# Group normalisation on one core: loops that begin at tile 0, padding on SyncE, and a sixth load cut into four gated parts

## The chip, the core and the metric

The kernel runs on one core of one Trainium2 chip. The metric is the device time of one execution in microseconds (us). The kernel before has a median of 633.02 us over three runs, between 632.91 and 633.99 us. A profile was taken of one further execution; the pages and the trace below are from it.

## What is computed

The input `x` has the shape 128 x 1024 x 32 x 16 in bf16. The 1024 channels of each of the 128 samples form 32 groups of 32 channels. Each group of each sample is normalised by its own mean and variance, and each channel is then scaled and shifted:

```
xr  = x.reshape(B, 32, C // 32, H, W)
mu  = xr.mean(axis=(2, 3, 4), keepdims=True)
var = ((xr - mu) ** 2).mean(axis=(2, 3, 4), keepdims=True)
xn  = ((xr - mu) / sqrt(var + 1e-5)).reshape(B, C, H, W)
out = xn * g[None, :, None, None] + b[None, :, None, None]
```

A group is 32 x 512 = 16,384 numbers, so one partition holds one group of one sample in one row of 32 KB, and 128 partitions hold the 32 groups of four samples.

## The kernel before, in words

The work is 32 tiles of 128 x 16,384 bf16 (4 MB each). Six buffers `xt0` to `xt5` hold them; tile i lives in buffer i mod 6, is normalised in place and is stored from there. Three small tables of ones, an identity matrix and a replication matrix are made at the start, and `g` and `b` (2 KB each) are loaded by ScalarE's queue and spread over the partitions by one small matmul (L143).

Each tile passes through the engines in this order. TensorE (PE) waits for the load (`ld[j]`, L155) and adds the 32 pieces of 512 columns with 32 matmuls against the identity (L157), which leaves 512 partial sums per row. VectorE (DVE) reduces them to minus the mean (`mean`, L176). ScalarE (ACT) squares the centred row in two halves with a running sum (L270, the two halves of one tile), and makes the standard deviation in two small instructions (L284, L291). VectorE inverts it (L189), forms scale and shift per channel (L192, L199), and applies them in 32 instructions of 512 columns (L209). VectorE runs `mean` one tile ahead: in the step of tile i it first does `mean(i + 1)`, then waits for the standard deviation of tile i.

SyncE (SP) issues every large transfer on one queue, in an order written out by hand (L112 to L139). It issues loads 0 to 5, then a *spacer* (`spacer`, L113 to L120: a load of 32 columns of 128 rows into a tile that nobody reads, 8 KB). Then it issues the stores in order, each after a wait for VectorE (`s_dve`). After stores 1, 4, 7, ... 25 it issues the next two or three loads, each after a wait for the store that frees its buffer (`st[j]`, L125), and after each such group one more spacer, which also waits for the spacer before it. In the steady part the queue thus holds, over and over, three stores, three loads and a spacer. There are 32 loads, 32 stores and 10 spacers. SyncE's program is written out in full, without a loop.

The other three engines run a loop of their own each (`loop`, L93 to L109). Tiles 0 and 1 (`HEAD = 2`) are written out ahead of it; then come five passes of six tiles. `head_slot={engine: 0}` puts the first instruction of the loop's body at the start of a block of the instruction memory; the engine jumps to it. At the end of a pass each engine waits until its own work has settled and takes the semaphores back by the pass's counts.

The lines that the change touches are the order of SyncE's queue (L111 to L139), the loop helper (L93 to L109), the waits' counts in the steps (L152 to L297), and the last wait for the spacers (L309).

Of the kernel before, what the change touches and what calls it, by code (L numbers as in the profile page):

```python
# [17 lines left out]
NBUF = 6  # L18
RUN = 3
MM_FREE = 512  # L20
HEAD = 2
SPARE = 32


@with_exitstack
def kernel(
# [7 lines left out]
    nc = tc.nc  # L34
    P = nc.NUM_PARTITIONS
# [6 lines left out]
    NT = B0 // NS  # L42
    KC = C // G
    F = KC * HW
    inv_n = 1.0 / float(F)
    NMM = F // MM_FREE
    TRIPS = (NT - HEAD) // NBUF
    assert F % MM_FREE == 0 and HEAD + TRIPS * NBUF == NT

    x_v = x.rearrange("(t n) (g k) h w -> t (n g) (k h w)", n=NS, g=G)  # L50
    o_v = out.rearrange("(t n) (g k) h w -> t (n g) (k h w)", n=NS, g=G)
# [6 lines left out]
    xt = [sb.tile([P, F], BF16, name=f"xt{j}") for j in range(NBUF)]  # L58
# [20 lines left out]
    def sem(name):  # L79
        return tc.alloc_semaphore(name)  # L80

    ld = [sem(f"ld{j}") for j in range(NBUF)]
    st = [sem(f"st{j}") for j in range(NBUF)]
    s_gb, s_set, s_eye, s_rep = sem("s_gb"), sem("s_set"), sem("s_eye"), sem("s_rep")
    s_pe, s_mean, s_sq, s_std = sem("s_pe"), sem("s_mean"), sem("s_sq"), sem("s_std")
    s_spare = sem("s_spare")
# [3 lines left out]
        j = i % NBUF  # L90
        return t[:, j : j + 1]

    def loop(engine, step, settle, counts):  # L93


        for i in range(HEAD):
            step(i)
        with nc.Fori(
            0,
            TRIPS,  # L100
            1,
            engines=bass.OrderedEngineSet([engine.engine]),
            head_slot={engine.engine: 0},
        ):
            for i in range(HEAD, HEAD + NBUF):
                step(i)
            settle()
            for s, n in counts:
                engine.sem_inc(s, -n)  # L109

    spacers = [0]  # L111

    def sync_program(sync):  # L113
        def spacer():

            n = spacers[0]
            spacers[0] += 1
            if n:
                sync.wait_ge(s_spare, 16 * n)
            sync.dma_start(out=spare[:], in_=x_v[0][:, 0:SPARE]).then_inc(s_spare, 16)  # L120

        def load(i):
            j = i % NBUF
            if i >= NBUF:
                sync.wait_ge(st[j], 16 * (i // NBUF))  # L125
            sync.dma_start(out=xt[j][:], in_=x_v[i]).then_inc(ld[j], 16)

        for i in range(min(NBUF, NT)):
            load(i)
        spacer()  # L130
        for i in range(NT):
            j = i % NBUF
            sync.wait_ge(s_dve, i + 1)
            sync.dma_start(out=o_v[i], in_=xt[j][:]).then_inc(st[j], 16)
            if (NT - NBUF - 1 - i) % RUN == 0 and i < NT - NBUF:
                for n in range(max(NBUF, i + 1 + NBUF - RUN), min(i + 1 + NBUF, NT)):
                    load(n)
                spacer()

    def tensor_program(pe):  # L140
        pe.wait_ge(s_gb, 32)
        pe.wait_ge(s_rep, 1)
        pe.matmul(  # L143
            out=gb_p[:].rearrange("p a k -> p (a k)"),
            lhsT=rep[:],
            rhs=gb_b[:].rearrange("q a k -> q (a k)"),
            start=True,
            stop=True,
        ).then_inc(s_pe, 1)
        pe.wait_ge(s_eye, 1)  # L150

        def step(i):  # L152
            j = i % NBUF
            pe.wait_ge(ld[j], 16)
            pe.sem_inc(ld[j], -16)  # L155
            for k in range(NMM):
                m = pe.matmul(  # L157
                    out=pa[j][:],
                    lhsT=eye[:],
                    rhs=xt[j][:, k * MM_FREE : (k + 1) * MM_FREE],  # L160
                    start=(k == 0),
                    stop=(k == NMM - 1),
                )
            m.then_inc(s_pe, 1)

        loop(pe, step, lambda: None, [])
        pe.drain()
        pe.sem_inc(s_pe, 1)

    def vector_program(dve):  # L170
        dve.memset(ones_b[:], 1.0).then_inc(s_set, 1)  # L171
        dve.tensor_copy(out=gb[:], in_=gb_p[:])._wait_ge(s_pe, 1).then_inc(s_dd, 1)  # L172
        gam, bet = gb[:, 0, :], gb[:, 1, :]

        def mean(i):
            dve.tensor_scalar(  # L176
                out=jd[i % 2][:],
                in0=pa[i % NBUF][:],
                scalar1=-inv_n,
                scalar2=None,  # L180
                op0=ALU.mult,
                op1=ALU.add,
                accum_out=col(negmean, i),
            )._wait_ge(s_pe, i + 2).then_inc(s_mean, 1)

        def step(i):
            j = i % NBUF
            mean(i + 1)
            dve.reciprocal(out=col(rstd, i), in_=col(std, i))._wait_ge(  # L189
                s_std, i + 1  # L190
            ).then_inc(s_dd, 1)
            dve.tensor_scalar(  # L192
                out=scl[j][:],
                in0=gam,
                scalar1=col(rstd, i),
                scalar2=None,
                op0=ALU.mult,
            )._wait_ge(s_dd, 3 * i + 2).then_inc(s_dd, 1)
            dve.scalar_tensor_tensor(  # L199
                out=bia[j][:],  # L200
                in0=scl[j][:],
                scalar=col(negmean, i),
                in1=bet,
                op0=ALU.mult,
                op1=ALU.add,
            )._wait_ge(s_dd, 3 * i + 3).then_inc(s_dd, 1)
            for k in range(KC):
                span = xt[j][:, k * HW : (k + 1) * HW]
                m = dve.tensor_scalar(  # L209
                    out=span,  # L210
                    in0=span,
                    scalar1=scl[j][:, k : k + 1],
                    scalar2=bia[j][:, k : k + 1],
                    op0=ALU.mult,
                    op1=ALU.add,
                )
                if k == 0:
                    m._wait_ge(s_dd, 3 * i + 4)
                if k == KC - 2 and i == HEAD + NBUF - 1:
                    m.then_inc(s_dd, 1)  # L220
            m.then_inc(s_dve, 1)

        def settle():
            dve.wait_ge(s_dd, 3 * (HEAD + NBUF) + 2)

        mean(0)
        loop(
            dve,
            step,
            settle,  # L230
            [(s_pe, NBUF), (s_std, NBUF), (s_dd, 3 * NBUF + 1)],
        )

    def pool_program(pool):
# [26 lines left out]
    def scalar_program(act):  # L261
        act.dma_start(out=gb_b[:, 0, :], in_=g_v).then_inc(s_gb, 16)
        act.dma_start(out=gb_b[:, 1, :], in_=b_v).then_inc(s_gb, 16)
        act.wait_ge(s_set, 2)
        act.activation(out=warm[:], in_=eps_t[:], func=ACT.Sqrt)  # L265

        def step(i):
            j = i % NBUF
            for h in range(2):
                m = act.activation(  # L270
                    out=ja[:],
                    in_=xt[j][:, h * F // 2 : (h + 1) * F // 2],
                    func=ACT.Square,
                    bias=col(negmean, i),
                    scale=1.0,
                    accum_out=sq[:, 2 * j + h : 2 * j + h + 1],
                    saturate=False,
                )
                if h == 0:
                    m._wait_ge(s_mean, i + 1)  # L280
                else:
                    m._wait_ge(s_sq, 3 * i + 1)
                m.then_inc(s_sq, 1)
            act.activation(  # L284
                out=col(half, i),
                in_=sq[:, 2 * j : 2 * j + 1],
                func=ACT.Identity,
                bias=eps_t[:],
                scale=inv_n,
            )._wait_ge(s_sq, 3 * i + 1).then_inc(s_sq, 1)  # L290
            act.activation(  # L291
                out=col(std, i),
                in_=sq[:, 2 * j + 1 : 2 * j + 2],
                func=ACT.Sqrt,
                bias=col(half, i),
                scale=inv_n,
            )._wait_ge(s_sq, 3 * i + 3).then_inc(s_std, 1)  # L297

        loop(act, step, lambda: act.drain(), [(s_mean, NBUF), (s_sq, 3 * NBUF)])

    with tc.tile_critical():  # L301
        with nc.Block() as block:
            block.sync(sync_program)
            block.tensor(tensor_program)
            block.vector(vector_program)
            block.gpsimd(pool_program)
            block.scalar(scalar_program)

        nc.sync.wait_ge(s_spare, 16 * spacers[0])  # L309
        for j in range(NBUF):  # L310
            nc.sync.wait_ge(st[j], 16 * len(range(j, NT, NBUF)))

# [29 lines left out]
```

## Time and profile before

| | |
|---|---|
| median of three runs | 633.02 us |
| the profiled execution, its own time | 633.55 us |
| its span, first to last instruction | 631.8 us |
| ACT busy | 476.2 us (75%) |
| DVE busy | 375.7 us (59%) |
| PE busy | 262.4 us (42%) |
| bytes moved by the DMA engines | 268.61 MB, a mean of 425 GB/s over the span |
| share of the DMA engines' time on the queue of the loads and stores (q1) | 99.0% |

The profile is one page of parts and a trace behind it that can be asked for views. In the page, part 2 cuts the span into 40 slices of 15.8 us; a digit is the busy share of a slice in tenths. Part 3 lists the DMA queues. Queues marked *instruction* carry pieces of the engines' programs. Part 6 lists transfers by line with the median time from issue to landing. The views used below are the timeline of one engine or queue, the waits of SyncE's queue, a table of stretches of time with the DMA engines' share in each, and the DMA queues in one stretch. The trace also keeps the completion marks of the transfers: a transfer leaves sixteen, one from each DMA engine that took part, with the time of each.

### The profile page before, as it was taken

What the parts mean: (1) busy time and instruction counts of PE and PEld (TensorE: products, weight loads), DVE (VectorE), ACT (ScalarE), POOL (GpSimd) and SP (SyncE); (2) the same over time, 40 slices, a digit from 0 to 9 for tenths busy, and PEclk for the clock granted to TensorE, in tenths of its full rate; (3) what the DMA queues carried; (4) which work ended last, traced back from release to release, by engine and by line L of the source; (5) the groups of instructions that cost most, each with busy time, mean ns of one, the idle gap of its engine ahead of it and who ended that gap; (6) DMA issues with size and microseconds to landing.
All of it is one profiled execution on the core that took longest, in us unless ns stands there. A gap on an engine that the chain in (4) does not pass through costs nothing. (4 is left out here: it accounts for less than half of the span.)

```text
span 631.8 us, 3680 instructions
## 1 busy us (share of the span) xinstructions
PE 262.4 (42%) x1025; PEld 106.8 (17%) x1025; DVE 375.7 (59%) x1188; ACT 476.2 (75%) x194; POOL 0.9 (0%) x7
## 2 busy tenths in 40 slices
PE   1987409009602850573077019404730680095000
PEld 0333103003200320231032003101310230032000
DVE  0057477775772677077727745771777177447771
ACT  0496999997994599289919964993899199749930
POOL 0000000000000000000000000000000000000000
PEclk9978858658855985687579559955975786598555
DMA  9999999999999999999999999999999999999986
GB/s 365 430 432 416 434 436 428 434 432 431 428 432 431 432 432 431 434 424 432 432 431 430 438 434 428 436 434 434 428 440 432 434 432 436 431 432 428 432 386 289
DMA packets 10760, 268.61 MB, mean 425 GB/s; under 512 B 2560, under 2 KB 2560, under 8 KB 2560
## 3 DMA queue, kind: packets, MB, share of 16 engines
q1 hardware_dynamic: 10656, 268.52, 99.0%
q8 instruction: 2, 0.03, 0.0%
q14 instruction: 6, 0.05, 0.0%
q10 hardware_dynamic: 96, 0.00, 0.0%
HBM read 134.30 MB, written 134.22 MB: 425 GB/s over the span
## 5 line engine op out<-in xcount | busy, mean ns | idle before, releaser
L270 ACT ACTIVATE ja<-xt,negmean 128x8192 fp8e5<-128x8192 bf16 x64 | 455.5, 7117 | 127.3 <-DVE jd L176 121.3
L157 PE MATMUL pa<-xt,eye 128*128 128x512 bf16 x1024 | 262.2, 421 | 307.4 <-PEq L155 305.2
L209 DVE TENSOR_SCALAR xt<-xt,scl,bia 128x512 bf16<-128x512 bf16 x1024 | 333.7, 407 | 1.2
L157 PEld LDWEIGHTS pa<-xt,eye 128*128 128x128 bf16 x1024 | 106.7, 106 | 462.5 <-issue 369.9
L176 DVE TENSOR_SCALAR_CACHE_REDUCE jd<-pa 128x512 bf16<-128x512 f32 x33 | 22.7, 687 | 143.5 <-PE pa L157 141.8
L189 DVE RECIPROCAL rstd<-std 128x1 f32<-128x1 f32 x32 | 5.2, 162 | 83.7 <-ACT std L291 83.7
L270 ACT ACTIVATION_READ_ACCUMULATOR ja<-xt,negmean 128x1 f32 x64 | 11.9, 186 | 0.0
L291 ACT ACTIVATE std<-sq,half 128x1 f32<-128x1 f32 x32 | 9.4, 295 | 1.0
L284 ACT ACTIVATE half<-sq,eps_t 128x1 f32<-128x1 f32 x32 | 8.9, 278 | 0.0
L199 DVE SCALAR_TENSOR_TENSOR bia<-scl,negmean,gb 128x32 f32<-128x32 f32 x32 | 8.1, 252 | 1.1
L192 DVE TENSOR_SCALAR scl<-gb,rstd 128x32 f32<-128x32 f32 x32 | 7.7, 242 | 1.1
L172 DVE COPY gb<-gb_p 128x64 f32<-128x64 f32 x1 | 0.2, 225 | 10.2 <-PE gb_p L143 10.2
L143 PE MATMUL gb_p<-gb_b,rep 32*128 32x64 bf16 x1 | 0.2, 228 | 11.2 <-DMA gb_b<-in_b_dram 11.2
L176 DVE DVE_READ_ACCUMULATOR jd<-pa 128x1 f32 x33 | 2.7, 83 | 0.0
L265 ACT ACT_TABLE_LOAD x1 | 1.3, 1283 | 1.9 <-issue 1.9
L143 PEld LDWEIGHTS gb_p<-gb_b,rep 32*128 32x128 bf16 x1 | 0.1, 97 | 11.2 <-DMA gb_b<-in_b_dram 11.2
L171 DVE MEMSET ones_b<- 128x128 bf16 x1 | 0.2, 165 | 1.1 <-SPq L301 1.1
L244 POOL TENSOR_SCALAR_AFFINE_SELECT rep<-ones_b 32x128 bf16<-32x128 bf16 x1 | 0.3, 302 | 0.0
L235 POOL TENSOR_SCALAR_AFFINE_SELECT eye<-ones_b 128x128 bf16<-128x128 bf16 x1 | 0.3, 293 | 0.8 <-DVE ones_b L171 0.8
L265 ACT ACTIVATE warm<-eps_t 128x1 f32<-128x1 f32 x1 | 0.2, 203 | 0.0
L253 POOL TENSOR_SCALAR eps_t<-ones_b 128x1 f32<-128x1 bf16 x1 | 0.2, 203 | 0.0
L326 POOL MEMSET const-bfloat16-1.0<- 128x1 bf16 x1 | 0.1, 102 | 0.0
(3 smaller groups left out, 0.3 us busy)
## 6 DMA issues: line engine op xcount, KB each, us to landing
xt<-in_x_dram SPq DMA_DIRECT2D x32, 4096.0 KB, 29.1
out_dram<-xt SPq DMA_DIRECT2D x32, 4096.0 KB, 33.0
spare<-in_x_dram SPq DMA_DIRECT2D x10, 8.0 KB, 29.1
gb_b<-in_g_dram ACTq DMA_DIRECT2D x1, 2.0 KB, 6.5
gb_b<-in_b_dram ACTq DMA_DIRECT2D x1, 2.0 KB, 9.7
```

The costliest lines, as they stand in the source:

```text
L143: pe.matmul(out=gb_p[:].rearrange("p a k -> p (a k)"), lhsT=rep[:], rhs=gb_b[:].rearrange("q a k -> q (a k)"), start=True, stop=True,).the ...
L157: m = pe.matmul(out=pa[j][:], lhsT=eye[:], rhs=xt[j][:, k * MM_FREE : (k + 1) * MM_FREE], start=(k == 0), stop=(k == NMM - 1),)
L176: dve.tensor_scalar(out=jd[i % 2][:], in0=pa[i % NBUF][:], scalar1=-inv_n, scalar2=None, op0=ALU.mult, op1=ALU.add, accum_out=col(negmean, i),
L189: dve.reciprocal(out=col(rstd, i), in_=col(std, i))._wait_ge(s_std, i + 1).then_inc(s_dd, 1)
L192: dve.tensor_scalar(out=scl[j][:], in0=gam, scalar1=col(rstd, i), scalar2=None, op0=ALU.mult,)._wait_ge(s_dd, 3 * i + 2).then_inc(s_dd, 1)
L199: dve.scalar_tensor_tensor(out=bia[j][:], in0=scl[j][:], scalar=col(negmean, i), in1=bet, op0=ALU.mult, op1=ALU.add,)._wait_ge(s_dd, 3 * i ...
L209: m = dve.tensor_scalar(out=span, in0=span, scalar1=scl[j][:, k : k + 1], scalar2=bia[j][:, k : k + 1], op0=ALU.mult, op1=ALU.add,)
L235: pool.affine_select(out=eye[:], in_=ones_b[:], pattern=[[-1, P]], compare_op=ALU.is_equal, fill=0.0, base=0, channel_multiplier=1,)._wait ...
L265: act.activation(out=warm[:], in_=eps_t[:], func=ACT.Sqrt)
L270: m = act.activation(out=ja[:], in_=xt[j][:, h * F // 2 : (h + 1) * F // 2], func=ACT.Square, bias=col(negmean, i), scale=1.0, accum_out=s ...
L284: act.activation(out=col(half, i), in_=sq[:, 2 * j : 2 * j + 1], func=ACT.Identity, bias=eps_t[:], scale=inv_n,)._wait_ge(s_sq, 3 * i + 1) ...
L291: act.activation(out=col(std, i), in_=sq[:, 2 * j + 1 : 2 * j + 2], func=ACT.Sqrt, bias=col(half, i), scale=inv_n,)._wait_ge(s_sq, 3 * i + ...
```

## The change

Four things change together.

1. `HEAD` goes. The three loops begin with tile 0, make five passes of six tiles, and tiles 30 and 31 are written out behind them. The waits count by the position in the pass. Only VectorE's loop keeps `head_slot`; those of TensorE and ScalarE begin wherever their program stands.
2. Load 5 is issued as four loads of 32 rows (rows c, c + 4, c + 8, ...; 1 MB each). Parts 0 and 1 are issued at once; part 2 waits until part 0 has landed, part 3 until part 1 has landed, and SyncE goes on only when part 2 has landed. A semaphore `ld_x` tells TensorE that the other parts are in; it is raised after every load into buffer 5.
3. Between parts 1 and 2 SyncE increments an otherwise unused semaphore 28 times (`PAD`).
4. The spacers go, all but one behind load 5.

```diff
-HEAD = 2
+PAD = 28
...
-    TRIPS = (NT - HEAD) // NBUF
+    TRIPS = (NT - 1) // NBUF
+    LOOPED = TRIPS * NBUF
...
-    def loop(engine, step, settle, counts):
-        for i in range(HEAD):
-            step(i)
+    def loop(engine, step, settle, counts, aligned=False):
         with nc.Fori(
...
-            head_slot={engine.engine: 0},
+            **({"head_slot": {engine.engine: 0}} if aligned else {}),
         ):
-            for i in range(HEAD, HEAD + NBUF):
-                step(i)
+            for j in range(NBUF):
+                step(j, j)
             settle()
             for s, n in counts:
                 engine.sem_inc(s, -n)
+        for i in range(LOOPED, NT):
+            step(i, i - LOOPED)
...
             sync.dma_start(out=xt[j][:], in_=x_v[i]).then_inc(ld[j], 16)
+            if j == NBUF - 1:
+                sync.sem_inc(ld_x, 1)
+
+        def load_gated(i):
+            j = i % NBUF
+            for c in range(4):
+                if c == 2:
+                    for n in range(PAD):
+                        sync.sem_inc(s_pad, 1)
+                if c >= 2:
+                    sync.wait_ge(qt[c - 2], 16)
+                rows = slice(c, P, 4)
+                sync.dma_start(out=xt[j][rows], in_=x_v[i][rows]).then_inc(
+                    qt[c] if c < 3 else ld[j], 16
+                )
+            sync.wait_ge(qt[2], 16)
+            sync.sem_inc(ld_x, 1)
 
-        for i in range(min(NBUF, NT)):
+        for i in range(NBUF - 1):
             load(i)
-        spacer()
+        load_gated(NBUF - 1)
+        sync.dma_start(out=spare[:], in_=x_v[0][:, 0:SPARE]).then_inc(s_spare, 16)
...
                     load(n)
-                spacer()
...
             pe.wait_ge(ld[j], 16)
             pe.sem_inc(ld[j], -16)
+            if j == NBUF - 1:
+                pe.wait_ge(ld_x, 1)
+                pe.sem_inc(ld_x, -1)
...
-        loop(pe, step, lambda: None, [])
-        pe.drain()
-        pe.sem_inc(s_pe, 1)
```

The last two lines gave VectorE's `mean(32)` its count; in the changed kernel `mean` is called only for tiles that exist, so VectorE does 32 of them in place of 33. The order of the loads and stores in the queue, the six buffers, the groups of three and every operation on a tile are the same.

## The prediction

> **What bounds the kernel now.** I read the page's slices first. The compute rows are far from full (ACT, the busiest, 75%), while the DMA row is full to the last two slices:
>
> ```profile
> DMA  9999999999999999999999999999999999999986
> GB/s 365 430 432 416 434 436 428 434 432 431 428 432 431 432 432 431 434 424 432 432 431 430 438 434 428 436 434 434 428 440 432 434 432 436 431 432 428 432 386 289
> ```
>
> So the stream of 64 transfers of 4 MB is the work to count. Its clean pace comes from the timeline of SyncE's queue, where the first load of each group is issued when a store has landed:
>
> ```profile
> 289.84 19.67 SPq L126 DMA_DIRECT2D xt<-in_x_dram  x3
> ...
> 348.02 19.64 SPq L126 DMA_DIRECT2D xt<-in_x_dram  x3
> ...
> 406.18 19.69 SPq L126 DMA_DIRECT2D xt<-in_x_dram  x3
> ...
> 465.17 19.68 SPq L126 DMA_DIRECT2D xt<-in_x_dram  x3
> ```
>
> Three stores, three loads and a spacer take 58.18 and 58.16 us, then 58.99: 9.695 us a transfer when clean (58.17 / 6), and 0.8 us lost once. 64 x 9.695 = 620.5 us. The first data packet starts at 2.05, so a stream without loss would land at 622.5. The last store lands at 630.3, where SyncE's last wait ends:
>
> ```profile
> SPq L311 <- DMA out_dram<-xt: 11.5, 1, 11.5
> ```
>
> (it began at 618.8). Some 7.8 us are lost, and the table of stretches, whose last three columns are granted clock, DMA share and GB/s, tells how:
>
> ```profile
> 600.00:612.00 12.00, 0.00 (x0) 0.00 (x0) 8.82 (x29) 6.42 (x4) 0.00 (x0) 0.50 1.00 431
> 612.00:618.50 6.50, 0.00 (x0) 0.00 (x0) 5.68 (x18) 0.00 (x0) 0.00 (x0) 0.50 0.46 197
> 618.50:628.30 9.80, 0.00 (x0) 0.00 (x0) 0.00 (x0) 0.00 (x0) 0.00 (x0) 0.50 1.00 429
> ```
>
> From 612 to 618.5 more than half of the 16 DMA engines are idle while the rest still carry store 30. The engines have drifted apart, and the last one sets each landing. The completion marks give the drift. Take the mark of each engine less 2.05 + 9.695 x (place in the queue), in us:
>
> ```
>                 load 0  load 2  load 4  load 5  load 7  load 10  load 13  load 16  load 22  load 25  load 29  load 31  store 30
> median engine    1.32    1.36    1.39    2.03    2.13    2.14     2.13     2.09     2.06     2.06     1.95     1.99     1.93
> last engine      1.77    3.07    3.11    4.54    4.59    5.51     5.56     6.50     6.61     7.39     7.38     7.73     7.78
> ```
>
> The median engine loses nothing after load 5. The last one loses 1.30 at load 2, 1.43 at load 5, and then 0.92, 0.94, 0.78 and 0.35 at loads 10, 16, 25 and 31: each time the last load of a group, when the engines ahead already write the next store. The loss at load 2 is a piece of TensorE's program, fetched as it reaches its loop; this is the queue part of the stretch 30.9 to 32.2 us:
>
> ```profile
> q1 hardware_dynamic: 31, 0.59, 108.0%
> q8 instruction: 1, 0.02, 4.8%
> ```
>
> 4.8% of 16 engines x 1.3 us is 1.0 us, all on one engine. A second such piece comes at 69.5 us, pieces of 8 KB (0.31 us each) at 57.4, 58.8, 63.9, 65.9, 115.4 and 622.5; these hit engines that were not last.
>
> **The change, part by part.** All terms are for the last engine, since it sets the end.
>
> *Spacers.* Nine go. On each engine a spacer is 8 packets of 11 ns and a mark of 9 ns: 97 ns, 9 x 0.097 = 0.87 us, in a queue that never rests. Bounds 0 and -0.87; I take **-0.87**. Their issue (0.43 us of SyncE each) costs nothing, as SyncE waits 367 us for VectorE in all.
>
> *The gate.* A part is two rows per engine, 2 x 1.213 us (the packet's duration in the trace) = 2.43 us. When part 0 has landed on the last engine, part 1 is already queued there. From a packet's end to its mark is 0.35 us, from mark to SyncE's next issue 0.02 (74.50 to 74.52 at the first gated load of before), from issue to first packet 1.0 (1.0 to 2.02 at load 0): 1.4 us, under 2.43. So the last engine does not rest: **0**. If that cover were gone, each of the three gates could cost it what is over 2.43. The engines ahead do rest, and come out at most 2.43 - 1.4 = 1.1 us ahead, where they were 2.5 ahead at load 5. SyncE stands in the gates until about 61 us; behind it stand the spacer and store 0, which VectorE has ready at 50.6. Store 0 lay behind load 5 in the queue anyway (it lands at 74.5, a store's 9.7 us after load 5's 64.8), so the later issue is hidden as long as load 5 takes no longer.
>
> *What the level field saves.* The four later losses sum to 0.92 + 0.94 + 0.78 + 0.35 = 2.99. Engines within about 1 us of the median lost nothing at those switches, and the field starts inside that. Bounds 0 and -2.99; I keep 0.4 for the drift that returns: **-2.6**. At load 5 itself the median engine lost 0.64 and the last 1.43; level engines should lose what the median did: **-0.8** (bounds 0 and -1.43).
>
> *Fetches.* TensorE's 16 KB piece stays: TensorE still reaches its second block while loads run, and 1.30 on one engine remains: **0** (bounds -1.30 if it meets an early engine and +1.30 if a second one falls behind the gate). ScalarE's pieces go with its jump. They cost it this:
>
> ```profile
> 59.14 7.12 ACT L270 ACTIVATE ja<-xt,negmean 128x8192 fp8e5<-128x8192 bf16 x1 [4.96 <-issue]
> ```
>
> but ScalarE's 5 us were hidden, since store 1 could not start before store 0 ended at 74: **0**. VectorE's two, and SyncE's (moved by the 28 increments to about 5 us, while loads 0 and 1 run), go ahead of the gate, which levels them. Behind it I allow one 8 KB piece, as the 622.5 us one: **+0.3**.
>
> *Small steps.* SyncE's increments of `ld_x`, TensorE's wait for it (raised before the load lands) and one `mean` less (0.69 us) lie under waits of tens of us: **0**.
>
> Sum: -0.87 - 2.6 - 0.8 + 0.3 = -4.0 us. The profiled execution had 633.55 us (span 631.8); it would be 629.55. The median lies 0.53 below the profiled execution, so I forecast **629.0**.
>
> What is late next? From load 29's landing (552.35) ScalarE's and VectorE's last three tiles take 65.4 us to the issue of store 31 (617.71), and an undelayed engine ends it 11.0 later (628.7). Load 29 comes 7.38 - (0.92 + 0.94 + 0.78 - 0.3) - 0.8 - 0.78 = 3.5 us behind the clean pace instead of 7.4, which puts that chain's end at 624.8. The DMA stream ends at 630.3 - 4.0 = 626.3, so the stream still decides, by 1.5 us.
>
> **A rule that speaks against it.** The row: queued transfers of 4 MB show no gap between them (58.17 us for six). The Trainium skill, "DMA: Bandwidth & Descriptors", section "Rules for kernel authors", advises large transfers over all 128 partitions and against cutting one by partitions; its section "Bandwidth" gives 6.15 us for 1 MB alone. By that four parts would last 24.6 us, an estimate, 15 us over the 9.7 us of load 5, if none overlapped. No run here shows a 1 MB transfer; two are always queued, so I leave that cost out of the sum.
>
> **Rivals.**
>
> *The drift is not what makes the late losses.* For it: at loads 7, 13, 22 and 28 the last engine, as far behind, lost next to nothing. Against: the median engine never lost. Then 0.87 remains, and at most 0.8 at load 5: 631.3 to 632.1.
>
> *A fetch falls behind the gate.* TensorE's last block may be reached at the end of its first pass or in the tiles behind the loop. One engine then loses 1.3 in a level field and drifts again by about 0.9: 629.0 + 2.2 = 631.2 at the worst, 630.3 if the drift stays out.
>
> *Slower: the rows of a part do not spread.* If the 32 rows, four partitions apart, meet two by two at the same place, a part takes 4.85 us instead of 2.43, load 5 lasts 19.4, and all behind it comes 9.7 us later: 638.7. It decides from 1.0 us more a part. For it: no transfer before has such rows, and even with 128 rows the 16 first packets took 1.8 to 2.5 us. Against: the two loads of 32 rows (`g`, `b`) left sixteen marks each, so 32 rows do use all engines.
>
> **How the numbers follow.** Level field 0.60 (its own range 627.4 to 630.4), fetch behind the gate 0.12, drift not the cause 0.13, parts slow 0.15. The range's low end takes the bounds: -0.87 - 2.99 - 1.43 - 1.30 = -6.6, or 626.4, of which I take 626.6; its high end the second rival and a little: 632.6. Left out: the slow parts. About 0.2% (1.3 us) is what a measurement of this kernel can tell from no change: 631.7 to 634.3. Faster is the first case, the second, and a third of the third: 0.76; same the rest of the third: 0.09; slower 0.15.
>
> **What the changed profile should show.** Load 5's four parts land about 2.4 us apart. At 612 to 618 the DMA share stays at 1.0 instead of 0.46. Group cycles are 58.1 us without one of 59. The last engine stays within about 1.5 us of the median from load 7 on. No stop of 5 us in ScalarE near 54. It is wrong if a part takes 3.4 us or more, if instruction packets lie behind 65 us, or if cycles of 59 us come back with level engines.

## The result and the profile after

The change makes the kernel slower. Its median is 635.66 us (six runs, 635.42 to 635.97) beside 632.96 us of the kernel before (six runs): a ratio of 1.0041, 95% interval 1.0028 to 1.0054, or 2.7 us. The forecast was 629.0 us, and the range ended at 632.6. The profiled execution has 635.74 us and a span of 634.0 us, against 633.55 and 631.8.

The page of the changed kernel, parts 2, 3 and 6, first the rows that answer to those of before:

```profile
DMA  8999999999999999999999999999999999999986
GB/s 364 429 429 402 430 418 407 432 430 430 430 430 440 432 430 438 436 428 434 430 430 430 438 433 430 432 436 434 430 432 432 430 432 438 432 429 434 431 387 271
q1 hardware_dynamic: 9408, 268.45, 98.6%
q8 instruction: 2, 0.03, 0.0%
q14 instruction: 6, 0.05, 0.0%
...
xt<-in_x_dram SPq DMA_DIRECT2D x4, 1024.0 KB, 28.7
```

The stream is as full as before (98.6% and 99.0%), and the bytes are nearly the same (268.45 MB and 268.52). But the sixth and seventh slices (79 to 111 us), which had 436 and 428 GB/s, have 418 and 407: a stretch just behind the gate. The timeline of SyncE's queue shows the gate and the group cycles:

```profile
3.77 55.23 SPq L134 DMA_DIRECT2D xt<-in_x_dram  x4
61.26 0.33 SPq L143 DMA_DIRECT2D spare<-in_x_dram  x1
...
289.69 19.84 SPq L119 DMA_DIRECT2D xt<-in_x_dram  x3
...
348.69 19.85 SPq L119 DMA_DIRECT2D xt<-in_x_dram  x3
...
407.96 19.85 SPq L119 DMA_DIRECT2D xt<-in_x_dram  x3
...
466.53 19.84 SPq L119 DMA_DIRECT2D xt<-in_x_dram  x3
```

The cycles are 59.00, 59.27 and 58.57 us, where before they were 58.18, 58.16 and 58.99: the losses inside the groups are still there, and larger. The clearest view is again the completion marks, each less 2.05 + 9.695 x (place in the queue), in us, median engine / last engine. This difference is called the *lag* below: how far an engine is behind the clean pace. Places count whole 4 MB transfers, so spacers are in the lag. The marks don't name their engine; "the last engine" is the last of the sixteen marks.

```
                     load 4     load 5     store 1    load 7     load 16    load 29     store 31
before               1.39/3.11  2.03/4.54  2.39/4.57  2.13/4.59  2.09/6.50  1.95/7.38   6.19/7.75
after                1.36/3.14  3.20/3.36  3.74/4.02  4.76/5.02  4.69/6.22  4.29/9.31   9.60/9.76
after, no gate (e4)  1.36/3.23  2.09/4.60  2.36/5.43  2.18/5.44  1.99/6.07  1.59/7.40   8.24/8.46
parts only (e15)     1.27/3.22  2.18/4.84  2.39/5.68  2.25/5.66  2.05/6.11  1.64/7.53   8.03/8.65
held, no parts (e16) 1.27/3.35  1.28/3.36  6.07/6.42  7.20/7.68  7.14/8.67  6.78/10.90  11.65/11.73
before, gate (e3)    1.30/2.78  3.02/4.00  3.60/5.53  4.50/7.22  4.59/7.83  4.42/9.12   8.37/9.41
```

The gate did level the engines: at load 5 all are within 0.4 us. From there to load 7 *every* engine loses 1.4 to 1.7 us (rank by rank). Then one engine goes behind again, by 4.29 us up to load 29 (9.31 - 5.02), where before the last one lost 2.79 over the same loads. At load 29 it is as far behind the median as before: 5.0 us, and 5.4 before. A table of stretches shows the first of these two; the last three columns are granted clock, DMA share and GB/s. First the kernel before, then the changed one:

```profile
79.00:85.00 6.00, 0.00 (x0) 0.00 (x0) 6.00 (x20) 5.97 (x3) 0.00 (x0) 0.50 0.99 426
99.00:105.00 6.00, 5.31 (x25) 2.26 (x24) 2.83 (x11) 5.97 (x5) 0.00 (x0) 1.00 1.04 438
```

```profile
79.00:85.00 6.00, 0.00 (x0) 0.00 (x0) 2.82 (x11) 5.97 (x5) 0.00 (x0) 0.50 0.90 362
99.00:105.00 6.00, 4.86 (x23) 2.05 (x22) 6.00 (x20) 5.97 (x3) 0.00 (x0) 1.00 0.98 350
105.00:111.00 6.00, 5.95 (x28) 2.65 (x27) 4.14 (x13) 6.00 (x1) 0.00 (x0) 1.00 1.01 437
```

At 99 to 105 us, where load 7 gives way to store 2, the engines are as busy as ever (0.98), yet move a fifth less: their packets are slower. Such a change from loads to stores, or from stores to loads, is called a *turn* below. What packets take over the usual 1.213 us ("slow packets") adds up to 1.02 us per engine there; it lies in the last two packets of load 7 on each engine, which start between 99.5 and 102 us. At 79 to 85 (store 1 to load 6) it is 0.38. Before, the same sums are 0.04 and 0.00 at these places, and 0.78 at 57 to 63 us, the first turn from loads to stores. The changed kernel pays nothing at that turn (median lag 3.20 at load 5, 3.29 at store 0); its 0.49 us near there, at 57 to 58.5, are the first packets after the rest in the gate.

The end, three stretches of the changed kernel:

```profile
600.00:612.00 12.00, 0.00 (x0) 0.00 (x0) 8.21 (x28) 9.81 (x6) 0.00 (x0) 0.50 0.96 410
612.00:618.50 6.50, 0.00 (x0) 0.00 (x0) 6.50 (x22) 0.00 (x0) 0.00 (x0) 0.50 0.77 333
618.50:628.30 9.80, 0.00 (x0) 0.00 (x0) 2.60 (x9) 0.00 (x0) 0.00 (x0) 0.50 0.76 328
```

The share at 612 to 618.5 is 0.77. The engines that are done stop for the same reason as before: store 31 can't be issued until VectorE has ended tile 31, which was at 617.7 and is now at 621.1. Before, the last engine went on with store 30 until 620.62, so this wait cost it nothing. Now it ends store 30 at 622.64, hardly later than the others can begin store 31, so the drifted engine and the chain of compute end together: in store 31 fifteen engines stand at 9.5 to 9.7 and the last at 9.76.

### The profile page after: what moved, and what is told of

Read it like the earlier page. It is cut to its first block, busy times and chain, and to the rows that moved or that the text cites. A ratio compares the mean times of both kernels' runs of the same rounds, so it can differ in the third digit from the quotient of the medians.

```text
span 634.0 us, 3690 instructions
## 1 busy us (share of the span) xinstructions
PE 259.5 (41%) x1008; PEld 106.5 (17%) x1025; DVE 375.1 (59%) x1186; ACT 476.6 (75%) x194; POOL 0.9 (0%) x7
## 3 DMA queue, kind: packets, MB, share of 16 engines
q1 hardware_dynamic: 9408, 268.45, 98.6%
## 5 line engine op out<-in xcount | busy, mean ns | idle before, releaser
L172 PE MATMUL pa<-xt,eye 128*128 128x512 bf16 x1007 | 259.2, 420 | 310.4 <-PEq L167 185.8
```

The lines of the kernel that those rows point to most:

```text
L172: m = pe.matmul(out=pa[j][:], lhsT=eye[:], rhs=xt[j][:, k * MM_FREE : (k + 1) * MM_FREE], start=(k == 0), stop=(k == NMM - 1),)
```

## The experiments

Sixteen kernels ran, each against the kernel before on the same chip, on five chips in all. "+" is this median less that of before on that chip, in us; for the change itself it is +2.7. The intervals reach 0.6 to 1.0 us either way, so a difference of a few tenths between two of these kernels tells nothing. Explanations set against each other: **L**, a level field loses time when all engines turn together from one direction to the other; **H**, the hold: SyncE stands in the gate, so the queue runs nearly empty; **S**, the spacers had shielded these turns. Beside these stand the pieces of the engines' programs that fall late, and, in the last two runs, the cut into parts as such.

### Spacers and gate, each on its own

**e1**, the changed kernel with its nine spacers back:

```diff
             if (NT - NBUF - 1 - i) % RUN == 0:
...
                     load(n)
+                if i < NT - NBUF:
+                    spacer()
```

> The changed kernel with the nine spacers put back behind each group of loads. Two theories. (S) The spacers keep the turn from loads to stores cheap; without them all engines lose 1.1 us at load 7 and the last engine 0.25 us at the first store of each group: with them back, about 635.7 - 1.1 - 7 x 0.25 + 0.9 for their own packets = 633.7 us or less, and no loss of all engines at load 7. (G) The gate makes all engines turn at the same moment, and a level field loses together: still 1.5 us lost by all engines at store 1 and load 7, and 635.7 + 0.9 = 636.6 us. (F) The places of the program fetches decide: also about 636.6 us.

Measured: 636.21, ratio 1.0046 [1.0032, 1.0059], +2.9. The loss behind the gate stays (load 7 at 5.00/5.29, slow packets 0.84 us per engine at 99 to 106), so S falls. The difference in time to the change, 0.2 us, is within what this can tell.

**e2**, the kernel before without its nine later spacers:

```diff
                     load(n)
-                spacer()
```

> The kernel before with the nine later spacers taken out and nothing else. (S) Slower by what the spacers shield: 633.0 + 7 x 0.25 + up to 1.1 - 0.9 = 633.9 to 634.9 us, with the last engine losing about 0.25 us at the first store of each group. (G) and (F) Faster by the spacers' packets: 633.0 - 0.9 = 632.1 us.

Measured: 634.16, ratio 1.0015 [1.0006, 1.0024], +0.8. No gain. The time is in the range that S gave, but S's sign is missing: no engine loses at load 7 (2.06/4.68). From load 7 to load 29 the median engine gains 0.16 us on that of before and the last 0.31, where the eight spacers of that stretch stood for 0.78 in the sum. In the profiled execution (633.57 us, 0.6 below the median) the last store lands 0.39 us earlier than before, at 629.89 against 630.28. But 1.95 us pass from there to the end of the span in place of 1.54: a piece of program that was fetched at 622.5 us before, by its place SyncE's, is now fetched at 631.5, behind the last landing.

**e3**, the kernel before with the gated load 5 and the 28 increments, all else as it was:

```diff
-        for i in range(min(NBUF, NT)):
+        for i in range(NBUF - 1):
             load(i)
+        load_gated(NBUF - 1)
         spacer()
```

> The kernel before with load 5 in four gated parts and the 28 increments, spacers and loops as before. (G) All engines level at load 5, and all lose about 1.5 us at store 1 and load 7: 633.0 + 1.5 = 634.5 us, less what the drift then spares. (S) and (F) No such loss with the spacers in place; the drift starts from a level field: 631 to 633 us.

Measured: 634.98, ratio 1.0026 [1.0015, 1.0036], +1.7. The gate costs on its own. In the table above its median engine loses 1.5 us between load 5 and load 7 as in the change (the last one 3.2, half of it by store 0). The slow packets are at the same two places: 0.43 us per engine at 79 to 86 and 0.97 at 99 to 106.

**e4**, the changed kernel with a plain load 5, without gate and increments:

```diff
-        for i in range(NBUF - 1):
+        for i in range(NBUF):
             load(i)
-        load_gated(NBUF - 1)
```

> The changed kernel with load 5 as one plain load, without the gates and the increments: the new loops and one spacer. (G) The loss at store 1 and load 7 goes: 635.7 - 1.5 = 634.2 us or less. (S) The loss stays with the missing spacers: 635 to 636 us. (F) The fetches lie elsewhere again, SyncE's near 115 us: between the two, with steps of the last engine at the fetches' times.

Measured: 634.77, ratio 1.0022 [1.0012, 1.0031], +1.5. The field is that of before, with no loss for the median engine behind load 5. So the gate and its increments are about 1.2 us of the 2.7, and about 1.5 come from the rest.

### Where the gate stands, and what holds the queue

**e5**, the changed kernel with load 4 gated in place of load 5, so that load 5 is queued behind the level field:

```diff
-        for i in range(NBUF - 1):
+        for i in range(NBUF - 2):
             load(i)
-        load_gated(NBUF - 1)
+        load_gated(NBUF - 2)
+        load(NBUF - 1)
```

> The changed kernel with load 4 in four gated parts in place of load 5, so that SyncE is free at about 51 us and store 0 is queued well ahead of load 5's end. Theory L (a level field loses together at its first turns): the engines are level at load 5 too; all lose 0.6 us there and about 0.4 at store 1 and 1.1 at load 7: about 635.7 us. Theory H (SyncE, held in the gates until 61 us, issues store 0 late, and the queue is short at the next turns): no loss of all engines at store 1 and load 7: about 634.5 us.

Measured: 636.44, ratio 1.0043 [1.0027, 1.0060], +3.0. The loss isn't at the places that L named, nor has it gone as H had it. It moves: 1.10 us per engine at load 5 to store 0, the first turn behind the gate, and nothing at loads 6 and 7 (load 5 at 4.90, load 7 at 5.05).

**e6**, the four parts without gates, SyncE held until three of them have landed:

```diff
-                if c >= 2:
-                    sync.wait_ge(qt[c - 2], 16)
...
-            sync.wait_ge(qt[2], 16)
+            for c in range(3):
+                sync.wait_ge(qt[c], 16)
```

> The changed kernel with load 5's four parts issued without the gates between them; SyncE still waits for parts 0, 1 and 2 before the spacer and store 0, so store 0 is issued at about 61 us as with the gates, but the engines are not made level. (L) No loss of all engines at store 1 and load 7: about 634.8 us, the time of the changed kernel without the gates. (H) The losses stay: about 635.7 us.

Measured: 635.40, ratio 1.0032 [1.0021, 1.0043], +2.0. L had expected no loss here, since it took the engines to stay apart. But the hold alone levels too: the engines ahead run out of work (median 1.40 at load 5, 2.87 at store 0, the last 3.33 and 3.35). Then two losses come at the same places, 0.85 and 0.89 us.

**e7**, the gates without the hold: store 0 is issued ahead of the wait for part 2:

```diff
-            sync.wait_ge(qt[2], 16)
-            sync.sem_inc(ld_x, 1)
...
             sync.dma_start(out=o_v[i], in_=xt[j][:]).then_inc(st[j], 16)
+            if i == 0:
+                sync.wait_ge(qt[2], 16)
+                sync.sem_inc(ld_x, 1)
```

> The changed kernel with the gates between the parts, but without the wait for part 2 ahead of store 0: store 0 is issued right behind part 3 at about 59 us, and the wait for part 2 follows it. The field is level, the hold is 2 us shorter. (L) The losses at store 1 and load 7 stay: about 635.7 us. (H) They shrink: 634.5 to 635.3 us.

Measured: 636.14, ratio 1.0039 [1.0025, 1.0053], +2.7. With a longer queue the loss is still paid, once, at load 5 to store 0 (1.17 us; load 5 at 4.26/5.30), and none later. So the length of the queue decides only *where* it falls: with the queue nearly empty the first turn is free and the next ones pay 0.4 and 1.0.

**e8**, the last part cut again, into 16, 8 and 8 rows, to set the engines half a part apart on purpose:

```diff
+            for rows, s in (
+                (slice(3, P, 8), qt[3]),
+                (slice(7, P, 16), qt[4]),
+                (slice(15, P, 16), ld[j]),
+            ):
+                sync.dma_start(out=xt[j][rows], in_=x_v[i][rows]).then_inc(s, 16)
```

> The changed kernel with part 3 issued as 16 rows, 8 rows and 8 rows: if 8 rows go to eight engines, and to the same eight both times, these carry three packets and the others one, so the level field is split by 2.4 us. (L) No loss of all engines at load 7; at most the eight late ones lose: 634.5 to 635.7 us. (H) The losses stay, and the late engines come on top: 636 to 637 us.

Measured: 640.10, ratio 1.0101 [1.0085, 1.0118], +6.7. The two loads of eight rows went to eight engines, so these have two rows more than the others, and store 0 lands between 3.67 and 8.06 us behind the pace. It doesn't save the turn: from load 6 to load 7 both halves, 2.5 us apart, still lose 0.6 to 0.9. L had expected no loss of all engines there; it can be kept only by saying that each half is level in itself.

### Pieces of program

**e9** and **e10**, the changed kernel with no increments and with 72:

```diff
-PAD = 28
+PAD = 0
```

> The changed kernel without the 28 increments, all else as in it. Theory P: the 28 increments did not bring SyncE's program piece ahead of the stores; they moved it from 622.5 us (before) to 372.6, where it cost the last engine 0.72 us. Without them the piece comes after 620 us and the step at load 20 goes: 635.7 - 0.7 = 635.0 us. Its rival: the step at load 20 has another cause, and the time stays at 635.7 us.

```diff
-PAD = 28
+PAD = 72
```

> The changed kernel with 72 increments in place of 28. SyncE's piece came at about its 80th instruction in both traces; with 72 the 80th lies among the increments, so the piece should be fetched at about 9 us, during load 0, ahead of the gates. Theory P: no step at load 20: about 635.0 us. Rival: 635.7 us.

Measured: 635.85, ratio 1.0042 [1.0028, 1.0056], and 635.23, ratio 1.0032 [1.0020, 1.0044]. The increments move SyncE's 8 KB piece. In the changed kernel it lies at 372.6 us, as the DMA queues in the stretch 372 to 373.2 show:

```profile
q1 hardware_dynamic: 16, 0.52, 103.2%
q14 instruction: 1, 0.01, 1.6%
```

1.6% of 16 engines x 1.2 us is 0.31 us, the piece. It hits the engine that is last: its lag rises by 0.72 us in load 20 (7.44 at store 16, 8.15 at load 20). With 72 increments the piece comes at 12.6 us and that step is gone (7.44 and 7.45). With none it comes at 627.3, in store 31, where the last engine stands 0.8 behind the others. Against the change, e9 is 0.2 us slower and e10 0.4 faster; both are within what this can tell.

**e11**, the kernel before with only VectorE's loop aligned:

```diff
-            head_slot={engine.engine: 0},
+            **({"head_slot": {engine.engine: 0}} if aligned else {}),
```

> The kernel before with the loops' alignment taken from TensorE and ScalarE and nothing else (tiles 0 and 1 stay ahead of the loops, spacers and plain load 5 stay). Theory T: the cost of the new loops is the turn of the loop between tiles 29 and 30, which stands in the last chain (0.4 us) and is not in this kernel: 632.5 to 633.5 us, as before. Rival: the places of the fetches cost it, and they move here too: 634 to 635 us.

Measured: 633.37, ratio 1.0004 [0.9995, 1.0013]. No difference.

**e12**, the kernel before with the 28 increments behind load 5:

```diff
+        for n in range(28):
+            sync.sem_inc(s_pad, 1)
         spacer()
```

> The kernel before with the 28 increments behind load 5 and nothing else. Theory P: SyncE's piece moves from 622.5 to about 370 to 400 us; if it meets the last engine the time rises by up to 0.7 us, to 634.0; if it meets another engine, 633.3 us as before.

Measured: 633.04, ratio 0.9999 [0.9990, 1.0008]. No difference, though the piece moves from 622.5 to 372.4 us here too: the last engine's lag shows no step there (6.54 at store 14, 6.50 at store 16).

### The gate in the middle of the run

**e13** and **e14**, the kernel before with load 9, or load 21, in four gated parts; the next load and the stores behind it wait for part 2. Load 5 is plain and the spacers stay:

```diff
+            if i == GATED:
+                for c in range(4):
+                    if c >= 2:
+                        sync.wait_ge(qt[c - 2], 16)
+                    rows = slice(c, P, 4)
+                    sync.dma_start(out=xt[j][rows], in_=x_v[i][rows]).then_inc(
+                        qt[c] if c < 3 else ld[j], 16
+                    )
+                sync.wait_ge(qt[2], 16)
```

> The kernel before with load 9 in four gated parts in place of a plain load; load 10 and store 5 follow ungated, load 5 is plain again. The median engine should come up to the last one, 4.6 us behind the clean pace, at load 9. Theory L (a level field loses at its next turn, wherever it is): all lose about 1.1 us at load 10, and with the usual drift the time is about 635 us. Theory E (only the first turns of a run cost): no loss of all engines at load 10; with the drift of 3 us seen behind the other gates about 634 us, and without it 631 us.

> The same with load 21 gated, where the last engine is 6.6 us behind the clean pace and the median 2. (L) All engines lose about 1.1 us at load 22: about 634.5 us. (E) None does; the last engine goes on from 6.6: if the level field drifts as behind the other gates (0.45 us a group) 8 us at load 29 and about 633.8 us, if it does not drift 6.5 us and 632.5 us.

Measured: 637.45, ratio 1.0062 [1.0048, 1.0076], +4.5, and 636.94, ratio 1.0048 [1.0035, 1.0061], +4.0. A loss follows the gate wherever it stands. Behind load 9 the last engine goes from 4.09 to 5.78 in load 9 and to 9.36 in load 10, the median from 2.18 to 4.19 and 6.82. Three stretches of e13: the beginning of load 10, its end ahead of the turn to store 5, and the time beyond:

```profile
151.00:157.00 6.00, 3.71 (x11) 1.30 (x10) 5.38 (x18) 4.75 (x1) 0.00 (x0) 0.73 0.95 355
157.00:163.00 6.00, 5.30 (x24) 2.16 (x22) 6.00 (x20) 5.97 (x3) 0.00 (x0) 0.99 1.02 350
163.00:169.00 6.00, 2.34 (x8) 0.92 (x9) 2.65 (x10) 5.97 (x5) 0.00 (x0) 0.87 1.02 433
```

Slow packets make 0.74 us per engine at 151 to 156 and 1.26 at 156 to 168, where before they make 0.14 at most. In e14 it is 0.65 and 1.10 at 384 to 405 us. The two parts are of different kinds. The first isn't a turn, as load 10 follows load 9: the engines run dry once more behind the last part (at 151.5 us four of sixteen carry a packet), and the first packet after this rest is slow, as the very first packets of the run are (0.78 us per engine at 2.0 to 2.5 us, before). The second part is the last two packets of load 10, ahead of the turn. Behind that turn the median engine loses nothing more, to the end.

### Level without parts, parts without level

Every kernel that lost behind its gate had both the level field and the four parts of interleaved rows. The last two take them apart. **e15**: the four parts issued at once, store 0 behind them without a hold. **e16**: one plain load 5, SyncE held until it has landed:

```diff
             for c in range(4):
-                if c >= 2:
-                    sync.wait_ge(qt[c - 2], 16)
...
             sync.dma_start(out=o_v[i], in_=xt[j][:]).then_inc(st[j], 16)
+            if i == 0:
+                for c in range(3):
+                    sync.wait_ge(qt[c], 16)
+                sync.sem_inc(ld_x, 1)
```

> The changed kernel with load 5 in the same four parts, but all four issued at once without a gate, and store 0 issued before SyncE waits for them, so that nothing holds the queue and the engines stay apart. If the loss behind load 5 comes from a level field, the median engine stays at about 2.2 us behind the clean pace at load 7 and the last at about 5.4, as without the parts, no stretch between 79 and 111 us falls to 350 GB/s, and the time is about 634.8 us. If the cut into parts makes the loss, the median engine is again at 4.5 us or more at load 7, and the time 635.4 us or more.

```diff
-            for c in range(4):
...
+            sync.dma_start(out=xt[j][:], in_=x_v[i]).then_inc(qt[0], 16)
+            sync.wait_ge(qt[0], 16)
+            sync.sem_inc(ld[j], 16)
             sync.sem_inc(ld_x, 1)
```

> The changed kernel with load 5 as one transfer, and SyncE held until all of it has landed, before store 0 is issued: no parts, but a level field at store 0, with a rest of about 1.4 us for the last engine. If a level field loses, the engines are level at store 0 at about 4.5 + 1.4 = 5.9 us behind the clean pace, and all of them lose another 1.0 to 1.4 us between store 1 and load 7, where the rate falls to 350 GB/s; load 7 is then at about 7.1 us, the time 636 us or more. If the cut into parts makes the loss, the engines stay at about 5.9 us through load 7, and the time is about 635 us.

Measured: e15 634.32, ratio 1.0015 [1.0006, 1.0024], +1.2; e16 637.95, ratio 1.0070 [1.0056, 1.0084], +4.8. The parts are free: e15's median engine stands at 2.25 at load 7, and no stretch behind 64 us is slow. The hold is not free: e16's engines have all rested (at 63.5 us none carries a packet), stand at 5.23 to 5.40 at store 0, all sixteen within 0.17 us, and lose 0.8 us at store 1 and 1.1 at load 7, at a DMA share of 0.97 and 0.90:

```profile
79.00:85.00 6.00, 0.00 (x0) 0.00 (x0) 2.82 (x10) 5.97 (x5) 0.00 (x0) 0.50 0.97 362
...
103.00:109.00 6.00, 4.65 (x23) 1.94 (x22) 6.00 (x20) 5.97 (x3) 0.00 (x0) 1.00 0.90 350
109.00:115.00 6.00, 4.88 (x23) 2.01 (x21) 2.82 (x11) 5.53 (x5) 0.00 (x0) 1.00 1.01 437
```

What these two runs don't show is that the *levelness* costs, as L says. In e15, without a gate or a hold, fourteen of the sixteen engines stand within 0.6 us of one another at load 7 (in e16 within 0.4) and lose nothing there; the same holds for e4. In the changed kernel all sixteen are within 0.7 us at load 10, as at load 7, and lose nothing. Another reading, found afterwards, fits all eighteen traces: the first turn from loads to stores at which the store is already queued, counted from the start of the run or from a rest of the engines, costs 0.8 to 1.3 us per engine in slow packets, and every later one 0.45 at most. It lies at load 5 in the kernel before (0.78), in e4, in e15 and, behind their gates, in e5 and e7; at load 7 in the change, e3, e6, e16 and also e8, whose field isn't level (0.8); and in e13 and e14 at load 5 and once more behind the gate. Where the hold left the queue nearly empty, the turn from stores to loads ahead of it costs 0.15 to 0.85 on top. No run has a rest and keeps the engines apart one by one, so this reading is better supported than L but not proven.

No kernel here beat the kernel before; e11 and e12 equal it.

## Why the prediction was wrong

**The bound** was right: the stream of 64 transfers and its last engine set the end, before and, now together with the chain of compute, after. The 7.8 us "lost" hold 1.3 that are no loss: the median engine's marks stand 1.32 behind 2.05 + 9.695 x place from load 0 on.

**The gate at 0** was right for its own stretch. The four parts land on the last engine at 56.09, 58.51, 61.18 and 63.58 us, 2.4 to 2.7 apart, and its lag rises by 0.2 us. SyncE's waits in the changed kernel:

```profile
SPq L134 <- DMA xt<-in_x_dram: 51.4, 2, 49.5
...
SPq L138 <- DMA xt<-in_x_dram: 2.2, 1, 2.2
```

They are hidden as forecast. The Trainium skill, "DMA: Bandwidth & Descriptors", section "Bandwidth", gives 6.15 us for a transfer of 1 MB (issued there from another engine, GpSimd). Parts queued behind one another don't show it here. The rival "rows of a part don't spread" falls with the same numbers.

**What the level field saves, -2.6, is the step that failed**, with its premise: "Engines within about 1 us of the median lost nothing at those switches, and the field starts inside that". It failed twice.

First, the turns behind the gate. The premise was read from a field that had paid at its first turn, at load 5 (0.78 us of slow packets per engine, 0.88 in e4, 1.06 in e15). A field that a gate or a hold has just let rest and levelled pays as much or more, later and on all sixteen engines: 1.1 to 1.2 us in e5 and e7, 1.4 in e3 and in the change, 1.7 to 2.0 in e6, e13, e14 and e16 (in e13 and e14 with the slow first packets of the next load). At load 5 itself the last engine gained more than the 0.8 forecast (3.36 against 4.54, -1.2), but at load 7 it stands at 5.02 against 4.59: all of it is given back, and 0.4 more.

Second, the drift came back, not to the 0.4 that was kept for it but in full. The trace of before could have told: the twelfth of its sixteen marks is 0.2 us behind the median at load 7 (2.30 against 2.13), 1.1 at load 13 and 3.5 at load 29 (5.48 against 1.95). So an engine within 1 us of the median does lose at those turns. Whatever the distance between last and median engine at load 7 (0.3 us in the change, 0.5 in e16, 2.5 before, 3.3 in e4), at load 29 it is 4.1 to 5.9 us in every one of these kernels: 5.4 before, 5.8 and 5.9 in e4 and e15, which didn't level, and 5.0, 4.7, 5.9, 4.5, 5.6 and 4.1 in the change, e3, e5, e6, e7 and e16, which did. Only e14, with eight loads left, is at 2.6. So the distance that the levelling took away grows back from load 13 on and is nearly all there at load 29, while what levelling and turns cost the *median* engine lasts to the end: 1.95 us before, 4.29 after, 2.34 more. 2.34 less 0.4 for the slightly smaller distance is the 1.93 us by which load 29 lands later on the last engine. This is read from the marks; those of e3, e5, e6, e7 and e16 show the same, the median raised for good and the distance grown back.

Of the steps by which one engine drifts in the change, these are seen: SyncE's piece, 0.72; 0.54 and 0.44 at loads 16 and 19, each the last of its group; and 0.23 to 0.26 at the first store of each of six groups from store 8 to store 23, 1.48 in all (0.30 before). e4 and e15 have hardly any of these small steps and drift by 1.96 and 1.87. What makes an engine drift was not found.

**Spacers, -0.87**, were mis-sized on the engine that counts: between load 7 and load 29, where eight of the nine stand (0.78 by the sum), it gains 0.31 us (e2 against before) and 0.24 (the change against e1). Taken out of the kernel before, they bought no time at all.

**Fetches, +0.3**: four pieces, not one, come behind the gate before the last store lands: at 80.1, 372.6, 568.4 and 600.5 us. SyncE's was expected near 5 us; it came at 372.6, since 28 increments moved it by far less than needed and 72 brought it to 12.6. So the increments didn't do what they were put in for. The piece at 80 also costs the unlevelled kernels: in e4 the last engine loses 0.78 between stores 0 and 1. The Trainium skill, "Runtime: NRT & Kernel Launch", section "Instruction fetch mechanics", calls the fetch hidden behind the engine's own issue rate. For the engine that executes, the kernel before shows one stop, ScalarE's 5 us at its jump. In a full stream the traces show another side, 0.7 us on the DMA engine that carries the piece.

**Small steps at 0** missed one. ScalarE's stop of 5 us has gone, as forecast. Its loop's end now lies between tiles 29 and 30, in the chain that ends last. The waits of ScalarE, then that chain in the changed kernel:

```profile
ACT ja L285 <- ACTq L314: 2.0, 5, 0.4
```

```profile
554.57 9.42 PE pa L172 x32
...
579.43 0.29 ACT std L306
579.72 0.04 ACTq L314
...
580.04 7.22 ACT ja L285 x2
```

and before, where the same step has no loop's end:

```profile
552.48 8.51 PE pa L157 x32
...
576.43 0.29 ACT std L291
576.73 7.12 ACT ja L270 x2
```

From the end of `std` to the next square it is 0.32 us instead of 0.02. From the landing of load 29 to the issue of store 31 it is 66.85 us instead of 65.4: 0.43 of that is ScalarE, 0.91 TensorE's first tile.

**What is late next** was answered with the chain 1.5 us ahead of the stream. Load 29 came at 9.31 in place of the forecast 3.5, so the chain moved with it, and both end together.

**The signs.** Right: the parts 2.4 us apart, no stop of ScalarE, the last engine near the median at load 7 (0.3 us, and 1.53 at load 16). Wrong: 5.0 us at load 29, the share of 0.77, the cycles of 59 us, the pieces behind 65 us. The prediction had named the last two as what would make it wrong. Of the rivals, none had a gate that costs all engines. The fetch behind the gate was the nearest: TensorE's 16 KB piece did come there (568.4 us), but no step of its size on the last engine follows it. One bound doesn't fit its words either: the range's high end is said to be the second rival and a little, but that rival gives 631.2 at the worst, and 632.6 lies 1.4 above it.

**What adds up to 2.7 us**, by medians: 1.2 for gate and increments (e4 to the change; alone, in e3, they cost 1.7) and 1.5 for the rest (before to e4), of which e2 shows 0.8 without the spacers and e11 nothing measurable for the alignment. The loops from tile 0 were not run alone; the 0.3 us of the loop's end are read from the trace, and the piece at 80 us belongs to them too.

The traces say more of this rest. The profiled execution of e4 is 1.25 us over that of before. Of this, 0.71 come ahead of the last landing: its last engine loses 0.78 at store 28, while a piece is fetched at 599.7 us, and the chain, with a first tile of 9.95 us, would end only 0.2 earlier. The other 0.54 come behind the landing, where two more pieces are fetched, at 632.1 and 632.8 us. This is so in all eighteen traces: from the last landing to the end of the span it is 1.53 to 1.56 us where no piece is fetched there, 1.69 to 1.95 with one (the change: 1.73) and 2.08 to 2.11 with two. That the pieces are the cause is read from these times; no run moved one of them alone.

Why the kernel before is slower without its spacers is thus answered only in part: the end is 0.4 us longer, but the landing came 0.4 earlier, with the chain of compute now ending the run (a first tile of 9.84 us in place of 8.51), and the median is 0.8 up. Open as well is why these turns are paid only once: in e16 fourteen engines still lie within 0.8 us of each other at load 29, and lose nothing at any later turn.

## What to carry to other kernels

In these runs, with sixteen DMA engines in a full stream of loads and stores, a gate or a hold that brought the engines level raised the median to the last one and cost all of them 1.1 to 2.0 us behind it, while the last drifted off again to about the same distance. Whether the levelness or the rest is what costs was not separated. Before a gate is put in to save what the last engine loses, ask what it costs the *median* engine, and keep the lags of both side by side. A small edit that moves program text should be followed to the place where the fetched piece lands: in the stream it cost only on the engine that was last, and there 0.7 us, and behind the last landing 0.2 to 0.4 us.

## What the runs showed of the hardware

*Slow turns at full share.* Ahead of the first full turn behind a gate, the DMA engines of the changed kernel are as busy as ever (0.98 of their time) and move 350 GB/s instead of 437 for some 6 us; the last two packets of the load on each engine are slow.

*TensorE's first tile behind an idle stretch varies.* Tile 29, 32 matmuls after some 30 us of idleness, took 8.38 us (e8) to 9.98 us (e10), in the chain that ends last. Here is the kernel before, where they take 8.51 us:

```profile
553.50:555.00 1.50, 1.50 (x5) 0.44 (x4) 0.00 (x0) 0.00 (x0) 0.00 (x0) 0.50 1.16 502
555.00:556.50 1.50, 1.50 (x7) 0.64 (x6) 0.00 (x0) 0.00 (x0) 0.00 (x0) 0.86 1.07 459
556.50:558.00 1.50, 1.50 (x8) 0.69 (x7) 0.00 (x0) 0.00 (x0) 0.00 (x0) 1.00 0.91 393
```

and the changed one, where they take 9.42 us:

```profile
555.00:556.50 1.50, 1.50 (x5) 0.54 (x4) 0.00 (x0) 0.00 (x0) 0.00 (x0) 0.50 1.06 459
556.50:558.00 1.50, 1.50 (x5) 0.50 (x4) 0.00 (x0) 0.00 (x0) 0.00 (x0) 0.50 0.86 371
558.00:559.50 1.50, 1.50 (x6) 0.53 (x5) 0.00 (x0) 0.00 (x0) 0.00 (x0) 0.56 1.12 481
```

The granted clock (third column from the right) goes from 0.5 to 1.0 some 3 us after the tile begins in the one and some 5 us in the other (2.5 in e8, 5.9 in e10); until then a matmul takes 427 ns, then 216. The Trainium skill, "TensorE: Matmul & The Clock Gate", section "Part 1: The HAM clock gate (the "warmup" mystery)", says that the number of slow matmuls varies from run to run because the window that measures activity runs freely. The traces agree that it varies (6 to 14 slow matmuls in this tile), and here 1.6 us of the end hang on it. It also says that the ramp costs less than 1% of a typical kernel's span. The 1.6 us are 0.25% of this one; but a change that is worth 0.4% can't ignore them.

*A load of eight rows used only eight of the sixteen engines* (e8: eight marks came as its data landed, in place of sixteen).
